# Rows of x stored tile by tile from SyncE's queue, and a group's gates by themselves

## The chip, the cores and the metric

The kernel runs on one core of a Trainium2 chip. The metric is the device time of one execution in microseconds (us). The engines of the core are TensorE (PE in the rows; its weight loads are PEld), VectorE (DVE), ScalarE (ACT), GpSimd (POOL) and SyncE (SP), which does nothing but issue transfers. Transfers (DMA) run on 16 DMA engines. SyncE's transfers form one hardware queue (q1 on the page), GpSimd's another one, made by software (q0).

## What is computed

Three layers in fp32, one after the other. Chunked attention (chunks of 64 tokens) gives the rows `x`, 4608 tokens of 512 numbers. A mixture of 8 experts takes one expert for each token that is not skipped and adds the expert's result, scaled with the gate. A last layer takes the maximum of three products and multiplies it with `w_out`.

```python
x = attn_out.transpose(0, 2, 1, 3).reshape(B * S, H * D)
e_idx = np.argmax(xc @ w_gate, axis=1)          # only where x @ w_skip > 0
gate_w = softmax(xc @ w_gate)[arange, e_idx]
y[mask] = gate_w[mask, None] * (np.maximum(xc[mask] @ w1[e], 0) @ w2[e])
out[do_compute] = xc + y
h = np.maximum(np.maximum(x @ w1, x @ w2), x @ w3)
return h @ w_out
```

## The kernel before

The first stage (up to about 165 us) is a loop over 36 tiles of 128 tokens, `for t in range(NT)`, in which the steps of several tiles overlap: round t loads q, k and v ahead, copies q and k into the order that TensorE wants (`pair_big`, on GpSimd), transposes them, makes the scores of tile t, transposes the exponentials of tile t-1, and multiplies those of tile t-2 with v. `scaled(t - 2)` then divides by the sums: on VectorE it writes the 128 rows of x of this tile (L361) into a buffer `xg` that holds the four tiles of a group, 128 x 4 x 520 numbers. The first tile of a group also has GpSimd clear the last seven columns of that buffer (L357). There are nine groups, and two such buffers: group 2 takes the buffer of group 0, group 3 that of group 1, and so on. `x_transpose(t - 2)` turns the rows for the routing (L374), and `logits` follows a round later.

When the four tiles of a group have their logits, `route(g)` and, a round later, `gates(g)` choose the experts; L432 writes the gate of each token into column 512 of the group's buffer. `store_x(g)` then writes the whole group, rows and gates, to `x_dram` with one transfer of GpSimd's (L546). In the rounds after that the slots of the group's tokens are sent with indirect transfers (`send_id`, L524), nine rounds after the tile. The ids so collected are read back by `load_ids` (L540) on SyncE: `ids_0` (the first columns of expert 0, wanted for the first gathers), the rest in `ids_sb`, and `ids_2` near the end. With these ids the second stage gathers rows of `x_dram` for each expert (L555); the first three tiles for expert 0 are gathered while the first stage still ends.

TensorE, VectorE, ScalarE and GpSimd run in the order in which the code is written (`manual_schedule`). SyncE's order is not written out: the scheduler places each transfer where its own model of time expects it to be ready. Each of SyncE's transfers uses one of eight completion semaphores in turn (DMAHW0 to DMAHW7 in the rows below), those of GpSimd DMASW0 to DMASW7.

A load of v of round t goes into one of eight buffers `v_all`, six rounds before it is used; loads of q and k go as far ahead.

Of the kernel before, what the change touches and what calls it, by code (L numbers as in the profile page):

```python
# [19 lines left out]
P = 128  # L20
B, H, S, D = 8, 8, 576, 64
N = B * S
DM = H * D
# [6 lines left out]
NT = N // P  # L30
# [10 lines left out]
def kernel(  # L41
# [15 lines left out]
    nc = tc.nc  # L57
# [5 lines left out]
    x_dram = dram.tile([N + 1, XW], F32, name="x_dram")  # L63
# [23 lines left out]
    def ps_sm(name):  # L87
        return ps("sm", name)
# [27 lines left out]
    def expert_src(e, i):  # L116
        if i < 4:
            return w1[e, i * P:(i + 1) * P, :], f"e{e}_{i}", (1, F1)
        r = (i - 4) * 2 * P
        return w2[e, r:r + 2 * P, :].rearrange("(a p) d -> p a d", p=P), f"e{e}_{i}", (2, DM)  # L120
# [67 lines left out]
    def pieces(t, end):  # L188
        got, t0 = [], t
        while t < end:  # L190
            b, s = divmod(t, WHOLE) if t < P * FULL else divmod(t - P * FULL, TAIL)
            n = min(end - t, (WHOLE if t < P * FULL else TAIL) - s)
            got.append((t - t0, b, s if t < P * FULL else s + WHOLE, n))
            t += n
        return got
# [54 lines left out]
    def load_v(t):  # L250
        for off, b, s, n in pieces(t * P, (t + 1) * P):
            link["load"] = nc.sync.dma_start(
                v_all[t % NV][off:off + n, :, :D], v[b, :, s:s + n, :].rearrange("h k d -> k h d"))
# [96 lines left out]
    def scaled(t):  # L350
        xp = units[t // 2]["xp", t % 2]
        g, j = PLACE[t]
        if j == 0:
            parts = [bpool.tile([P, GT, XW], F32, tag="xg", name=f"xg{g}")]
            groups[g] = parts, apool.tile([P, GT, E + 1], F32, tag="lg", name=f"lg{g}")
            for part in parts:
                nc.gpsimd.memset(part[:, :, DM + 1:], 0.0)  # L357
        sm = apool.tile([P, 2, 4], F32, tag="sm", name=f"sm{t}", bufs=3)
        nc.vector.tensor_scalar_add(sm, xp[:, :, :, D], 1e-9)
        nc.vector.reciprocal(sm, sm)  # L360
        nc.vector.tensor_tensor(  # L361
            rows_of(t)[:, :DM].rearrange("p (h r d) -> p r h d", h=4, r=2), xp[:, :, :, :D],
            sm.unsqueeze(3).to_broadcast([P, 2, 4, D]), op=ALU.mult)

    def rows_of(t):
        g, j = PLACE[t]
        part, i = divmod(j, groups[g][0][0].shape[1])
        return groups[g][0][part][:, i, :]
# [12 lines left out]
    def logits(t):  # L381
        g, j = PLACE[t]
        lp = ps_sm(f"lp{t}")[:, :R]
        for c in range(KC):
            link["logits", t] = nc.tensor.matmul(lp, xt[t][:, c, :], wcat[:, c, :], start=c == 0, stop=c == KC - 1)
        units["lp", t] = lp

    def logits_out(t):
        g, j = PLACE[t]
        nc.scalar.copy(groups[g][1][:, j, :], units["lp", t])  # L390
# [29 lines left out]
    def gates(g):  # L420
        parts, nt = groups[g][0], SIZES[g]
        T = slice(0, nt)
        ex, m8, comp = routing[g]
        oh, eo = picks[g]
        sm = apool.tile([P, GT], F32, tag="rsm", name=f"rsm_{g}", bufs=1)
        nc.vector.reduce_sum(sm[:, T], ex[:, T], axis=AX)
        nc.vector.tensor_scalar(eo[:, T], m8[:, T], float(-COLS), float(E * COLS + P * SLOTS), op0=ALU.mult, op1=ALU.add)
        nc.vector.tensor_scalar_add(sm[:, T], sm[:, T], 1e-9)
        nc.vector.scalar_tensor_tensor(eo[:, T], comp[:, T], float(-P * SLOTS), eo[:, T], op0=ALU.mult, op1=ALU.add)
        for i, part in enumerate(parts):  # L430
            n = part.shape[1]
            nc.vector.reciprocal(part[:, :, DM], sm[:, i * n:i * n + n])  # L432
        store_x(g)
        before, after = run[g % 2], run[(g + 1) % 2]
        got = apool.tile([P, E], F32, tag="rgot", name=f"rgot_{g}", bufs=1)
        nc.vector.reduce_sum(got, oh[:, T].rearrange("p t e -> p e t"), axis=AX)
        nc.vector.tensor_tensor(after, before, got, op=ALU.add)
# [101 lines left out]
    def load_ids(dst, which, cols, eng=nc.sync):  # L539
        follow(eng.dma_start(dst, ids_rows[which][:, cols]), sent[which], "slots are written in any order")  # L540

    def store_x(g):
        r = START[g] * P
        for part in groups[g][0]:
            n = part.shape[1] * P
            nc.gpsimd.dma_start(x_dram[r:r + n, :].rearrange("(t p) c -> p t c", p=P), part)  # L546
            r += n

    def apart(ins, own, other):
# [203 lines left out]
    def last_of(t):  # L753
        return PLACE[t][0] if 0 <= t < NT and PLACE[t][1] == GT - 1 else None

    def weights_ahead(t):
        for i, at, *_ in ROUND:
            if at == t:
                src, name, shape = expert_src(0, i)
                with tc.issue_after(link["load"].ins):  # L760
                    if i in STAGED:
                        a = shape[0]
                        nc.sync.dma_start(raws_0[i].rearrange("p (a b) -> p a b", a=a) if a > 1 else raws_0[i], src)
                    else:
                        raws_0[i] = load_raw(src, name, shape)
# [15 lines left out]
    for t in range(NT):  # L781
        u, s = divmod(t, 2)
        ranked = last_of(t - 5)
        if ranked is not None:
            rank_out(ranked)
        if t - LAG in late:
            send_id(t - LAG)
        if t == 0:
            load_qk(5)
        if s == 0 and u + 6 < SLOW + 2 * len(BIG):  # L790
            load_qk(u + 6)
        units.setdefault(u, {})
        if t >= 1 and t - 1 not in vm:
            cross(t - 1)
        if t == NT - 2:
            cross(NT - 2)
            cross(NT - 1)
        for group in PAIR.get(t, ()):
            (pair_big if len(group) > 2 else pair_heads)(*group[:2])
        if t == 8:  # L800
            nc.gpsimd.tensor_copy(tok_f, tok_i)
            nc.gpsimd.tensor_scalar_add(tok_f, tok_f, float(-N))
            nc.gpsimd.iota(col_i, pattern=[[1, P]], base=0, channel_multiplier=0)
            nc.gpsimd.tensor_copy(col_f, col_i)
        if t >= 2:
            values(t - 2)
            scaled(t - 2)
            if t - 2 + NV < NT:
                load_v(t - 2 + NV)
        weights_ahead(t)  # L810
        if t in (33, 34):
            with tc.issue_after(link["load"].ins):
                raws_1[EARLY[t - 33]] = load_raw(*expert_src(1, EARLY[t - 33]))
        scores(t)
        shift(t)
        if t >= 1:
            exp_transpose(t - 1)
        for group in TURN.get(t, ()):
            (turn_big if len(group) > 2 else qk_transpose)(*group[:2], "q")
        if t >= 1:  # L820
            cross_up(t - 1)
        if t >= 3:
            logits(t - 3)
            logits_out(t - 3)
        for group in TURN.get(t, ()):
            (turn_big if len(group) > 2 else qk_transpose)(*group[:2], "k")
        exponentials(t)
        g = last_of(t - 3)
        if g is not None:
            route(g)  # L830
        if t >= 2:
            x_transpose(t - 2)
            x_out(t - 2)
        g = last_of(t - 4)
        if g is not None:
            gates(g)
            rank_of(g)
        g = ranked
        if g is not None:
            if g == 2:  # L840
                count_first()
            place(g)
            if g == FIRST:
                late = range(START[g + 1], NT)
                fill_first(run[(g + 1) % 2][:, 0:1])
                xgs[0] = [four_kb([P, XW], F32, f"xg_0_{j}") for j in range(2)]
                rows = START[g + 1] * P
                fetch = t + 6
        if fetch is not None and t - fetch in (-4, -3):
            for i in range(2):  # L850
                send_id(START[FIRST] + 2 * (t - fetch + 4) + i)
            if t == fetch - 3:
                load_ids(ids_0, 0, slice(0, 3))
        rounded(t)
        rests(t)
        if t == fetch:
            at = cpool.tile([P, 2], I32, name="at")
            nc.vector.tensor_single_scalar(at, ids_0[:, :2], rows - 1, op=ALU.min)
            for j in range(2):
                gather(xgs[0][j], at[:, j:j + 1], rows)  # L860
# [5 lines left out]
        send_id(t)  # L866
    values(NT - 2)
    scaled(NT - 2)
    logits(NT - 3)
    logits_out(NT - 3)  # L870
    exp_transpose(NT - 1)
# [7 lines left out]
    load_ids(ids_sb, 0, slice(0, SLOTS))  # L879
    values(NT - 1)  # L880
    scaled(NT - 1)
    logits(NT - 2)
    logits_out(NT - 2)
    rounded(36)
# [450 lines left out]
    for b, (r0, n) in enumerate(BLOCKS):  # L1335
# [31 lines left out]
        for half in range(2):  # L1367
            for i in range(n // P):
# [11 lines left out]
                r = r0 + half * n + i * P  # L1380
# [34 lines left out]
```

## Time and profile before

| | us |
|---|---|
| median of 3 runs | 1050.54 (1046.76 to 1053.8) |
| the profiled execution | 1043.47 |
| its span, first to last instruction | 1041.8 |
| TensorE busy | 999.0 (96%) |
| VectorE busy | 575.4 (55%) |
| ScalarE busy | 420.2 (40%) |
| GpSimd busy | 315.6 (30%) |

Busy times are those of one profiled execution; its own time stands in the second row, beside the median of the runs that were timed. In a row of a timeline the first number is the start of the instruction in us from the span's start, the second its duration. The clock of TensorE is given as a share of full speed, 2.4 GHz; 0.50 is 1.2 GHz. The share of DMA is the mean busy share of the 16 engines, and can be over 1 where packets of two queues overlap.

### The profile page before, as it was taken

The page shows a single profiled execution, that of the slowest core. Times are in us where ns is not written, and L with a number is a line of the kernel's source. Part 1 is how long each engine was busy: PE and PEld are TensorE (multiplying, and loading weights), DVE is VectorE, ACT ScalarE, POOL GpSimd, SP SyncE. Part 2 cuts the span into 40 slices and gives each one's busy share as a digit, 9 for nine tenths or more (in the row PEclk, how much of TensorE's full clock was granted, in tenths as well). Part 3 has the DMA queues.
Part 4 walks back from the last instruction along what each step waited for, and adds up shares of the span by engine and source line. Part 5 has one row for each costly group of instructions (what it writes and reads, how often), then busy time and mean ns, then how long its engine had stood idle before and what let it go on. Part 6 is the DMA issues. An engine that isn't in the chain of part 4 may idle for free.

```text
span 1041.8 us, 19679 instructions
## 1 busy us (share of the span) xinstructions
PE 999.0 (96%) x7569; PEld 855.2 (82%) x7569; DVE 575.4 (55%) x1100; ACT 420.2 (40%) x762; POOL 315.6 (30%) x359
## 2 busy tenths in 40 slices
PE   8998999998989999899999999999999999999996
PEld 7988988888777888787878887788888888878995
DVE  4676888688273795655898524343344424434241
ACT  5876874455251554424443422223222322223230
POOL 3665867512120343105321502213012311103010
PEclk9998999999999999999999999999999999999999
DMA  9999973877281795659995446645566356674771
GB/s 235 295 307 293 238 237 111 260 248 272 87 284 62 250 329 200 234 188 349 339 319 169 149 142 185 192 132 172 162 193 190 103 168 200 185 222 156 224 232 40
DMA packets 198258, 217.44 MB, mean 209 GB/s; under 512 B 47195, under 2 KB 162027, under 8 KB 198144
## 3 DMA queue, kind: packets, MB, share of 16 engines
q1 hardware_dynamic: 185328, 176.27, 55.7%
q0 software_dynamic: 10224, 31.40, 8.7%
q10 hardware_dynamic: 2592, 8.26, 2.1%
q8 instruction: 70, 1.15, 0.5%
q14 instruction: 44, 0.36, 0.1%
HBM read 175.30 MB, written 41.98 MB: 209 GB/s over the span
## 4 chain that ended last, share of the span: by engine, by line
PE 51%; DMA 3%; DVE 2%; issue 0%; ACT 0%; SPq 0%; DVEq 0%; ACTq 0%
PE f_a L663 6%; PE f_a L665 6%; PE f_a L664 6%; PE o L663 5%; PE o L665 5%; PE o L664 5%; PE f_d L663 3%; PE f_d L665 3%; PE f_d L664 3%; DMA ws<-m_sums 2%; PE f_b L663 2%; PE f_b L665 2%; PE f_b L664 2%; PE trf L1124 1%; DMA x<-x_dram 1%; PE h L663 0%
## 5 line engine op out<-in xcount | busy, mean ns | idle before, releaser
L94 POOL TENSOR_TENSOR fh<-best,fh 128x512 fp32r<-128x512 f32 (+1 forms) x60 | 75.2, 1260 | 358.1 <-ACT fh L93 271.1
L663 PE MATMUL f_a<-x_t,ws 128*128 128x512 f32 (+1 forms) x270 | 100.3, 372 | 0.8 <-DVE best L1298 0.8
L665 PE MATMUL f_a<-x_t,ws 128*128 128x512 f32 (+1 forms) x270 | 99.6, 369 | 0.0
L664 PE MATMUL f_a<-x_t,ws 128*128 128x512 f32 (+1 forms) x270 | 99.5, 369 | 0.0
L664 PE MATMUL o<-wlo_m,fh 128*128 128x512 f32 x216 | 84.6, 392 | 0.0
L663 PE MATMUL o<-whi_m,fh 128*128 128x512 f32 x216 | 84.5, 392 | 0.0
L665 PE MATMUL o<-whi_m,fh 128*128 128x512 f32 x216 | 83.4, 393 | 0.0
L943 POOL DMA_INDIRECT x_dram<-xg,ids_sb x20 | 30.0, 1501 | 172.5 <-DVE xg L941 81.0
L93 ACT CAST whi_e<-raw_e 128x1024 fp32r<-128x1024 f32 x56 | 58.2, 1051 | 58.8 <-DMA raw_e<-in_moe_w_dram 39.0
L663 PE MATMUL h<-xhi,whi_e 128*128 128x256 f32 x256 | 73.5, 287 | 7.9 <-PEq L1240 2.8
L94 DVE TENSOR_TENSOR wlo_e<-raw_e,whi_e 128x1024 fp32r<-128x1024 f32 x56 | 68.0, 1222 | 20.6 <-ACT whi_e L93 20.2
L663 PE MATMUL y<-whi_e,hhi 128*128 128x512 f32 x184 | 74.0, 403 | 0.9 <-ACT hhi L1012 0.9
L93 ACT CAST fh<-best 128x512 fp32r<-128x512 f32 (+1 forms) x60 | 34.5, 579 | 95.0 <-DVE best L1300 58.3
L664 PE MATMUL h<-xlo,whi_e 128*128 128x256 f32 x256 | 72.5, 283 | 0.2 <-issue 0.2
L665 PE MATMUL y<-whi_e,hlo 128*128 128x512 f32 x184 | 72.5, 397 | 0.2
L665 PE MATMUL h<-xhi,wlo_e 128*128 128x256 f32 x256 | 72.5, 283 | 0.0
L664 PE MATMUL y<-wlo_e,hhi 128*128 128x512 f32 x184 | 72.2, 393 | 0.0
L1130 POOL TENSOR_TENSOR x_t<-t,x_t 128x512 fp32r<-128x512 f32 (+1 forms) x40 | 46.1, 1182 | 50.9 <-ACT x_t L1129 50.9
L1303 ACT COPY p<-f_a 128x512 f32<-128x512 f32 (+1 forms) x45 | 24.3, 543 | 87.0 <-PE f_a L665 86.8
L663 PEld LDWEIGHTS f_a<-x_t,ws 128*128 128x128 f32 x270 | 51.0, 189 | 9.9 <-DVE best L1298 1.6
L665 PEld LDWEIGHTS f_a<-x_t,ws 128*128 128x128 f32 x270 | 50.9, 189 | 8.6
L663 PEld LDWEIGHTS h<-xhi,whi_e 128*128 128x128 f32 x256 | 49.2, 192 | 10.7 <-issue 9.3
(242 smaller groups left out, 2604.8 us busy)
## 6 DMA issues: line engine op xcount, KB each, us to landing
ws<-m_sums SPq DMA_DIRECT2D x135, 512.0 KB
raw_e<-in_moe_w_dram SPq DMA_DIRECT2D x64, 512.0 KB
ws<-m_sums SPq DMA_DIRECT2D x45, 256.0 KB
x_dram<-xg POOLq DMA_DIRECT2D x9, 1040.0 KB, 6.5
x<-x_dram SPq DMA_DIRECT2D x36, 256.0 KB
v_all<-in_v_dram SPq DMA_DIRECT2D x32, 256.0 KB
out_dram<-os SPq DMA_DIRECT2D x32, 256.0 KB
m_sums<-n_raw ACTq DMA_DIRECT2D x18, 448.0 KB
```

The costliest lines, as they stand in the source:

```text
L93: nc.scalar.copy(hi, src),
L94: eng.tensor_tensor(lo, src, hi.bitcast(F32), op=ALU.subtract),
L663: nc.tensor.matmul(acc, ahi, bhi, start=first, stop=False, skip_group_check=onto)
L664: nc.tensor.matmul(acc, ahi, blo, start=False, stop=False, skip_group_check=onto)
L665: return nc.tensor.matmul(acc, alo, bhi, start=False, stop=last, skip_group_check=onto)
L943: ins = nc.gpsimd.indirect_dma_start(out=x_dram[:, :], out_offset=bass.IndirectOffsetOnAxis(ap=ids, axis=0), in_=xg, in_offset=None, bound ...
L1124: nc.tensor.transpose(tr[:, i * P:(i + 1) * P], row[:, c * P:(c + 1) * P], ident)
L1130: eng.tensor_tensor(lo, src, hi.bitcast(F32), op=ALU.subtract)
L1303: nc.scalar.copy(p1, acc_a)
```

## The change

`store_x(g)`, one transfer of 1040 KB for each group on GpSimd, is gone. In its place `store_tile(t)` writes the 512 columns of x of one tile (256 KB), on SyncE, and is called behind `scaled` of this tile, 36 times. `store_gates(g)` writes the last eight columns (the gate and the seven cleared ones) of a group's 512 rows, 16 KB in pieces of 32 bytes, on SyncE, at the place where `store_x` was called.

```diff
--- before.py
+++ after.py
@@ -430,7 +430,7 @@
         for i, part in enumerate(parts):
             n = part.shape[1]
             nc.vector.reciprocal(part[:, :, DM], sm[:, i * n:i * n + n])
-        store_x(g)
+        store_gates(g)
         before, after = run[g % 2], run[(g + 1) % 2]
         got = apool.tile([P, E], F32, tag="rgot", name=f"rgot_{g}", bufs=1)
         nc.vector.reduce_sum(got, oh[:, T].rearrange("p t e -> p e t"), axis=AX)
@@ -539,11 +539,15 @@
     def load_ids(dst, which, cols, eng=nc.sync):
         follow(eng.dma_start(dst, ids_rows[which][:, cols]), sent[which], "slots are written in any order")
 
-    def store_x(g):
+    def store_tile(t):
+        nc.sync.dma_start(x_dram[t * P:t * P + P, :DM], rows_of(t)[:, :DM])
+
+    def store_gates(g):
         r = START[g] * P
         for part in groups[g][0]:
             n = part.shape[1] * P
-            nc.gpsimd.dma_start(x_dram[r:r + n, :].rearrange("(t p) c -> p t c", p=P), part)
+            nc.sync.dma_start(
+                x_dram[r:r + n, DM:].rearrange("(t p) c -> p t c", p=P), part[:, :, DM:])
             r += n
 
     def apart(ins, own, other):
@@ -807,6 +811,7 @@
             scaled(t - 2)
             if t - 2 + NV < NT:
                 load_v(t - 2 + NV)
+            store_tile(t - 2)
         weights_ahead(t)
         if t in (33, 34):
             with tc.issue_after(link["load"].ins):
@@ -866,6 +871,7 @@
         send_id(t)
     values(NT - 2)
     scaled(NT - 2)
+    store_tile(NT - 2)
     logits(NT - 3)
     logits_out(NT - 3)
     exp_transpose(NT - 1)
@@ -879,6 +885,7 @@
     load_ids(ids_sb, 0, slice(0, SLOTS))
     values(NT - 1)
     scaled(NT - 1)
+    store_tile(NT - 1)
     logits(NT - 2)
     logits_out(NT - 2)
     rounded(36)
```

The scheduler places the new transfers in SyncE's line. These are SyncE's rows in the first stage, around the load of `v_all5` for tile 13, before (xg0 is the buffer of group 0, xg1 that of group 1):

```order
L252 DMA v_all4_138<-in_v_dram 128x8x64
L222 DMA qt10_927<-in_q_dram 128x4x256
L222 DMA kt10_928<-in_k_dram 128x4x256
L252 DMA v_all5_139<-in_v_dram 128x8x64
L222 DMA qt11_1121<-in_q_dram 128x4x256
L222 DMA kt11_1122<-in_k_dram 128x4x256
L252 DMA v_all6_140<-in_v_dram 128x8x64
L252 DMA v_all7_141<-in_v_dram 128x8x64
```

The same place after the change:

```order
L252 DMA v_all4_138<-in_v_dram 128x8x64
L543 DMA x_dram_66<-xg1_738 128x512
L222 DMA qt10_933<-in_q_dram 128x4x256
L222 DMA kt10_934<-in_k_dram 128x4x256
L252 DMA v_all5_139<-in_v_dram 128x8x64
L543 DMA x_dram_66<-xg1_738 128x512
L549 DMA x_dram_66<-xg0_374 128x4x8
L222 DMA qt11_1129<-in_q_dram 128x4x256
L222 DMA kt11_1130<-in_k_dram 128x4x256
L252 DMA v_all6_140<-in_v_dram 128x8x64
L543 DMA x_dram_66<-xg1_738 128x512
L252 DMA v_all7_141<-in_v_dram 128x8x64
```

Stores of tiles of group 0 (128x512, from xg0) and of group 1 (from xg1) now stand between the loads, and the gates of group 0 (L549, 128x4x8) stand two places behind the load of `v_all5`.

On VectorE the order stays. What changes is what tile 8, the first of group 2, waits for. Before (the names in brackets are semaphores):

```order
L359 TENSOR_SCALAR sm8_1151<-xp8_1131 128x8 [waits PE_49]
L360 RECIPROCAL sm8_1151<-sm8_1151 128x8 [waits DVE_49]
L361 TENSOR_TENSOR xg2_1148<-xp8_1131,sm8_1151 128x2x4x64 [waits DMASW5_49,DVE_49,Pool_49]
L313 TENSOR_REDUCE mx10_1173<-sc10_1156 128x8 [waits PE_49]
L315 TENSOR_TENSOR ex10_1175<-sc10_1156,mx10_1173 128x2x4x64 [waits DVE_49,Activation_49]
```

After:

```order
L359 TENSOR_SCALAR sm8_1159<-xp8_1139 128x8 [waits PE_49]
L360 RECIPROCAL sm8_1159<-sm8_1159 128x8 [waits DVE_49]
L361 TENSOR_TENSOR xg2_1156<-xp8_1139,sm8_1159 128x2x4x64 [waits DMAHW4_49,DMAHW3_49,DMAHW5_49,DMAHW1_49,DMAHW7_49,DVE_49,Pool_49]
L313 TENSOR_REDUCE mx10_1182<-sc10_1165 128x8 [waits PE_49]
L315 TENSOR_TENSOR ex10_1184<-sc10_1165,mx10_1182 128x2x4x64 [waits DVE_49,Activation_49]
```

L361 waited for one transfer of GpSimd's and now waits for five of SyncE's, the four stores of tiles of group 0 and its gates. The maxima of round 10 (L313) stand behind it, as before.

The last place is SyncE's line at the end of the first stage. Before:

```order
L100 DMA raw_e1_1_3557<-in_moe_w1_dram 128x1024
L540 DMA ids_0_121<-ids_dram0_67 128x3
L540 DMA ids_sb_118<-ids_dram0_67 128x288
L540 DMA ids_2_120<-ids_dram1_68 128x1
L616 DMA n_raw0_4513<-in_moe2_w1_dram 128x2x512
```

After:

```order
L100 DMA raw_e1_1_3590<-in_moe_w1_dram 128x1024
L540 DMA ids_0_121<-ids_dram0_67 128x3
L540 DMA ids_sb_118<-ids_dram0_67 128x288
L543 DMA x_dram_66<-xg7_3209 128x512 x2
L549 DMA x_dram_66<-xg6_2800 128x4x8
L543 DMA x_dram_66<-xg7_3209 128x512 x2
L543 DMA x_dram_66<-xg8_3582 128x512 x2
L549 DMA x_dram_66<-xg7_3209 128x4x8
L543 DMA x_dram_66<-xg8_3582 128x512
L540 DMA ids_2_120<-ids_dram1_68 128x1
L543 DMA x_dram_66<-xg8_3582 128x512
L549 DMA x_dram_66<-xg8_3582 128x4x8
```

The stores of tiles 28 to 34 (from xg7 and xg8) and the gates of groups 6 and 7 now stand behind the loads of `ids_0` and `ids_sb`, and the store of tile 35 and the gates of group 8 behind that of `ids_2`.

## Rows read from the trace of the kernel before

**Rows 1.** The page: span, and busy time of the engines.

```profile
span 1041.8 us, 19679 instructions
PE 999.0 (96%) x7569; PEld 855.2 (82%) x7569; DVE 575.4 (55%) x1100; ACT 420.2 (40%) x762; POOL 315.6 (30%) x359
```

**Rows 2.** Stretches: length, busy time (instructions) of each engine, clock, DMA.

```profile
core 0: us, PE busy (x) PEld busy (x) DVE busy (x) ACT busy (x) POOL busy (x), PEclk, DMA share, GB/s
...
40.00:64.00 24.00, 22.71 (x490) 21.50 (x489) 17.54 (x58) 18.09 (x41) 14.68 (x28) 1.00 1.04 296
...
92.00:99.00 7.00, 7.00 (x92) 6.55 (x90) 4.55 (x15) 3.58 (x9) 1.41 (x3) 0.51 1.02 247
```

**Rows 3.** Timeline of SyncE: start, duration of the issue, line, transfer.

```profile
27.76 2.50 SPq L222 DMA_DIRECT2D qt<-in_q_dram  x1
30.36 1.28 SPq L222 DMA_DIRECT2D kt<-in_k_dram  x1
...
57.56 1.06 SPq L252 DMA_DIRECT2D v_all<-in_v_dram  x1
...
72.26 1.64 SPq L100 DMA_DIRECT2D raw_e<-in_moe_w_dram  x1
...
89.84 1.57 SPq L100 DMA_DIRECT2D raw_e<-in_moe_w_dram  x1
...
156.09 0.34 SPq L540 DMA_DIRECT2D ids<-ids_dram  x1
...
175.27 0.32 SPq L540 DMA_DIRECT2D ids<-ids_dram  x1
```

**Rows 4.** Timeline of GpSimd; in brackets its idle time before, and what ended it.

```profile
34.79 0.61 POOL L233 COPY qr<-qt 128x512 f32<-128x512 f32 x1 [2.00 <-DMA qt<-in_q_dram]
36.89 0.61 POOL L233 COPY kr<-kt 128x512 f32<-128x512 f32 x1 [1.49 <-DMA kt<-in_k_dram]
...
44.70 0.78 POOL L546 DMA_DIRECT2D x_dram<-xg  x1
...
55.13 0.12 POOL L357 MEMSET xg<- 128x28 f32 x1 [0.26 <-DMA x_dram<-xg]
...
148.83 0.81 POOL L546 DMA_DIRECT2D x_dram<-xg  x1 [4.77 <-DVE run L437]
...
184.34 1.06 POOL L555 DMA_INDIRECT xg<-x_dram,ids  x1 [0.30 <-issue]
```

**Rows 5.** Timeline of VectorE, L361 of tiles 8, 12, 16 and 32.

```profile
55.20 0.69 DVE L361 TENSOR_TENSOR xg<-xp,sm 128x512 f32<-128x512 f32 x1 [0.54 <-DMA x_dram<-xg]
...
70.78 0.69 DVE L361 TENSOR_TENSOR xg<-xp,sm 128x512 f32<-128x512 f32 x1 [0.18 <-DMA x_dram<-xg]
...
88.48 0.69 DVE L361 TENSOR_TENSOR xg<-xp,sm 128x512 f32<-128x512 f32 x1
...
158.20 0.69 DVE L361 TENSOR_TENSOR xg<-xp,sm 128x512 f32<-128x512 f32 x1
```

**Rows 6.** Timeline of TensorE: tile 8 turned, and two idle times.

```profile
56.82 0.60 PE L374 MATMUL trx<-ident,xg 128*128 128x128 f32 x4
...
71.40 0.57 PE L306 MATMUL sc<-kT,qT 64*64 64x64 f32 x22 [1.26 <-issue]
...
90.88 0.21 PE L306 MATMUL sc<-kT,qT 64*64 64x64 f32 x1 [2.50 <-issue]
```

**Rows 7.** Waits of GpSimd to 150, TensorE to 156 us: total, times, longest.

```profile
POOL x_dram L546 <- DVE run L437: 20.1, 6, 4.8
...
PE sc L306 <- issue: 6.0, 4, 2.5
```

**Rows 8.** Instructions on x_dram: the stores, duration min/median/max, and the landing.

```profile
L546 POOL DMA_DIRECT2D x_dram<-xg x9: 778/802/821, 44.7 to 177.0; - x9
...
DMA to landing us min/median/max: 3.0/6.5/8.2
```

## The prediction

> **What bounds the kernel now.** I read the page first: the span is 1041.8 us and TensorE is busy in 999.0 of it [rows 1], so the kernel ends when TensorE's work ends, and the change can cost or bring only what it adds to or takes from TensorE's idle time. The change touches the first stage alone (attention and routing, up to about 185 us). There, the table of stretches says that the 16 DMA engines are full: from 40 to 64 us their share is 1.04 at 296 GB/s [rows 2]. The list of waits says who was late: GpSimd waited 20.1 us before its stores of x, always for `run` of L437, the end of the gates [rows 7], but that cost nothing, since none of TensorE's groups in that list waits for GpSimd: TensorE's idle time from 26 to 156 us stands in three groups there, all ended by nothing that the profile shows ("issue"), the largest 6.0 us in 4 places before the scores [rows 7]. The two largest are 1.26 us at 71.4 and 2.50 us at 90.9 [rows 6]; after the second the clock is at 0.51 from 92 to 99 [rows 2], which costs 7.0 x (1 - 0.51) = 3.4 us more. Last, the timelines of SyncE, GpSimd and VectorE give the times of the single steps [rows 3 to 5].
>
> The place to look at is the buffer of a group. `xg` has two buffers, so group 2 takes that of group 0, and neither its first scaled tile (L361, tile 8) nor its memset (L357) can start before the stores of group 0 have landed. Before, this is just met: GpSimd's store is issued at 44.70, and the memset at 55.13 and L361 at 55.20 come after a wait of 0.26 and 0.54 us for its landing [rows 4, 5]. For group 3 the wait is 0.18 us, at 70.78, for group 4 there is none [rows 5].
>
> **What the change removes.** Nine stores on GpSimd, 0.80 us each, 7.2 us together [rows 8], and the 20.1 us of waiting ahead of them. GpSimd's next work (slots' stores, copies of q, k and v) comes that much earlier, but nobody waited for it: 0. At the seam to the experts the same holds: the gather of the third tile starts at 184.34 right behind GpSimd's last send, with 0.30 us of idle time that ends by itself [rows 4], so an earlier store moves nothing. I put 0; the bound above is what GpSimd's rows before it hold, 0.80 us.
>
> **What it adds and moves.** 36 stores of 256 KB and 9 of 16 KB in SyncE's line, which is in order. The store of tile t waits for L361 of tile t only, the gates' for L432. The rows of the order show that the gates of group 0 now stand two places behind the load of `v_all5`, though what they hold is ready three of the loop's rounds before it is needed. And that load is issued only at 57.56 [rows 3], 2.4 us after the moment when group 2 needs the buffer. So SyncE's line runs behind the loop here, and GpSimd's own queue did not. This is the step on which the forecast rests:
> Issue: 57.56 + 1.06 for the load's own issue [rows 3] + about 0.4 for the store of tile 5 (the short issues are 0.32 to 0.34 [rows 3]) = 59.0. The line also carries more ahead of it: six tile stores, 6 x 0.262 = 1.57 MB, where the GpSimd store had moved 1.06 MB through the same engines; 0.51 MB more at 296 GB/s [rows 2] is 1.7 us. Bounds 59.0 (if two queues at once had cost the engines as much) and 60.7; I take 60.0.
> Landing: of SyncE's loads two show it, since GpSimd waited for them: issued at 27.76 and 30.36, used at 34.79 and 36.89 [rows 3, 4], so 7.0 and 6.5 us for half a megabyte, of which its own bytes are 0.52 / 296 = 1.8 us. Small gates behind a full line: 4.7 to 5.2. The gates are 512 pieces of 32 bytes, which no row before shows; the nearest is a load of v in 1024 pieces, whose issue took 1.06 us [rows 3], so half of that, 0.5 us, is in the bounds that follow. Below stands the shortest landing of any transfer of x_dram, 3.0 us [rows 8], above 7.0. I take 4.5.
> So group 0's gates land at 64.5 (62.0 to 67.7), and L361 of tile 8 starts there and not at 55.20: 9.3 us late (6.8 to 12.5).
>
> The Trainium skill's page "DMA: Bandwidth & Descriptors", section "Queues, rings and completion order", says that an engine takes one queue's descriptors in ring order and goes round robin between queues. By that rule the store in GpSimd's own queue passed the loads, and the gates in SyncE's cannot; the rows agree. The same page ("Anatomy of one DMA") prices a transfer at 2.0 us plus its bytes at 436 GB/s; by it the gates would land at 62.0 and the wait be 6.8 us, and the sum 6.5. The 6.5 and 7.0 us of the rows are longer, and they decide.
>
> What hangs on L361: VectorE works in order, so the maxima and differences of round 10 stand behind it; TensorE transposes tile 8 at 56.82, 0.9 us after L361 ends at 55.89 [rows 5, 6], and the next exponentials' transposes come behind that. Neither has more than that 0.9 us to give, and the DVE, ACT and PE steps of the next round start from L361 too. All 9.3 us are TensorE's.
>
> The clock: a gap of 2.50 us was followed by half the clock, 3.4 us [rows 2, 6]. One of 7 to 9 us can do the same; bounds 0 and 3.4, I take 2.6. Against it, the gaps of 1.26 and 2.50 us and the 3.4 us of half clock (7.2 in all) stand in the profile of before; after the stop SyncE's line is some 9 us nearer to the loop, so they may go. They end by no engine's work, and the engines stay as full as at 40 to 64 us, so I credit a little under half, 3.4; bounds 0 and 7.2.
>
> Later groups: the gates of group 1 stand behind the load issued at 72.26 [rows 3] and the store of tile 9: 72.26 + 1.64 + 0.4 + about 1 (the shift chosen above) + 4.5 = 79.8, needed at 70.78 + 9.3 = 80.1 [rows 5]. Those of group 2 stand behind 89.84 [rows 3]: 89.84 + 1.57 + 0.4 + 1 + 4.5 = 97.3, needed at 88.48 + 9.3 = 97.8. Both are met by the first stop, barely: 0.5 for the two together (0 to 3).
>
> Near the end, the stores of tiles 28 to 31 and the gates of group 6 stand behind the load of `ids_0`, issued at 156.09 [rows 3]. It waits for slots whose sends stood behind the megabyte store at 148.83 [rows 4]. Without this store they leave some 5 us earlier, so the gates land before L361 of tile 32 at 158.20 [rows 5]. If not, 156.09 + 0.8 + 3.0 = 159.9, 1.7 us late. I put 0. The store of tile 35 and the last gates stand behind `ids_2`, issued at 175.27 [rows 3]: 175.27 + 0.8 + 7.0 = 183.1 at the latest landing, before the gather at 184.34.
>
> **Sum**: 9.3 + 2.6 - 3.4 + 0.5 = +9.0 us. The profiled execution took 1043.47 us (the span and 1.7 us around it), so it would take 1052.5. It is 7.1 us under the median of the runs, 1050.54; on that the forecast is 1059.5. A measurement of this kernel tells about 1% (10.5 us) from no change, so this is just inside.
>
> **Rivals.** (1) The stop recurs. If tile stores cost the engines more than loads of the same size, the line falls further behind at groups 3 and 4. A store that takes 1.5 us in place of 0.9 adds 0.6 x 4 = 2.4 us a group, and with the first wait at its upper bound this is 12.5 + 2.4 + 2.4 + 2.6 - 3.4 = +16.5: 1067. For it: both later groups are met by under 1 us. Against: from group 2 on the loop is 9 us later, and so is every need.
> (2) The stop comes but is paid back: 6.8 + 0 - 7.2 = about 0, 1050. It needs TensorE's gaps to hang on how far SyncE's line is behind; nothing in the rows says so.
> (3) Faster. Without the megabyte bursts of GpSimd's queue the loads flow better, the gates land by 55.2, and the gaps of 71.4 and 90.9 go with their half clock: -7.2, 1043; with the other two places of the 6.0 us, -9.4. The point that decides is the landing of group 0's gates: 57.56 + 3.0 is over 55.2 already, so SyncE's line must be at least 5 us further at this place than it was, with more bytes in it. The same page of the Trainium skill ("Issuing engine by pattern") gives plain stores to SyncE as generally faster; no row here shows it for a line that is full.
> (4) No change at all, since the loop needs the buffer later than I read: excluded by the 0.54 us wait at 55.20.
>
> **How the numbers follow.** Forecast (one stop, +4 to +13): 0.68. Rival 1: 0.12. Rival 2: 0.12. Rival 3: 0.08. The range goes from rival 2 (1050) to rival 1 (1067). Over 1061.0 lie rival 1 and two fifths of the forecast: 0.40. Under 1040.0 lies most of rival 3: 0.06. The rest is 0.54.
>
> **What will show it.** VectorE's L361 of tile 8 and the memset ahead of it should end a wait of 7 to 12 us for a transfer of x_dram at 62 to 68 us, TensorE's largest gap in the first stage should be there, with half the clock behind it, and groups 3 to 8 should wait under 2 us each. The gather of the third tile should start 7 to 12 us after 184.34, and no wait of TensorE's should be new at the seam. The forecast is wrong if L361 of tile 8 starts before 60 us, if a later group's wait is longer than group 2's, or if SyncE is no longer behind the loop at `v_all5`.

## The result and the profile after

The changed kernel takes 1051.05 us (median of 22 runs), the kernel before 1046.1 us in the runs beside it (median of 22). The ratio of the two is 1.0077, 95% interval [1.0058, 1.0096]: of 1046.1 us that is 8.1 us (6.1 to 10.0). The plain difference of the two medians, 4.95 us, lies under that interval, so 5 to 8 us is taken for the cost below, and up to 10 can't be excluded. It is under the 1% that, by the prediction, a measurement tells from no change; over 22 runs of each kernel the interval excludes 1 all the same. The forecast was 1059.5, which is +9.0 us on the 1050.54 known then: of its 8.45 us too much, 4.4 are the change of the median before, and the rest is a sum that was some 1 to 4 us too high; against the interval alone, +9.0 is not off.

The profiled execution after took 1049.09 us, 5.6 more than that of before. The page after: span, busy times, and the two large queues (packets, MB, share of 16 engines).

```profile
span 1047.3 us, 19780 instructions
PE 999.4 (95%) x7569; PEld 856.0 (82%) x7569; DVE 573.9 (55%) x1100; ACT 419.8 (40%) x762; POOL 309.7 (30%) x350
...
q1 hardware_dynamic: 195264, 185.86, 57.7%
q0 software_dynamic: 7776, 21.81, 6.4%
```

TensorE's busy time is nearly the same, 999.4 us for 999.0 [rows 1], and the span is 5.5 us longer: by this page 5.1 of it is idle time. Work at the half clock counts as busy, for as long as it then takes, so the page doesn't show what the clock cost. SyncE's queue (q1) now carries the rows of x too. GpSimd's busy time fell by 5.9 us, which gained nothing.

The timeline of SyncE after (start, duration of the issue, line, transfer): the load of `v_all5`, the store of tile 5, the gates of group 0, then the gates of groups 1 and 2, and the load of `ids_0`.

```profile
56.25 1.03 SPq L252 DMA_DIRECT2D v_all<-in_v_dram  x1
57.37 1.46 SPq L543 DMA_DIRECT2D x_dram<-xg  x1
58.91 0.39 SPq L549 DMA_DIRECT2D x_dram<-xg  x1
...
73.03 0.38 SPq L549 DMA_DIRECT2D x_dram<-xg  x1
...
89.85 0.38 SPq L549 DMA_DIRECT2D x_dram<-xg  x1
...
153.71 0.34 SPq L540 DMA_DIRECT2D ids<-ids_dram  x1
```

Before, GpSimd had sent the rows and gates of group 0 at 44.70 [rows 4]. Now the gates of this group leave at 58.91, behind the load of `v_all5`, as the order had shown. GpSimd's timeline after: the last copy ahead of the memset, the memset of group 2's buffer, and the gather of the third tile.

```profile
53.03 0.61 POOL L233 COPY kr<-qkt 128x512 f32<-128x512 f32 x1
63.83 0.12 POOL L357 MEMSET xg<- 128x28 f32 x1 [10.18 <-DMA x_dram<-xg]
...
187.77 1.04 POOL L559 DMA_INDIRECT xg<-x_dram,ids  x1 [0.30 <-DVE hlo L706]
```

The memset ends a wait of 10.18 us for a transfer of `x_dram`, where before it had waited 0.26 us [rows 4]. So the gates landed at about 63.8, 4.9 us after their issue. VectorE's timeline after, L361 of tiles 8, 12, 16, 20, 32 and 35:

```profile
64.05 0.69 DVE L361 TENSOR_TENSOR xg<-xp,sm 128x512 f32<-128x512 f32 x1 [9.65 <-DMA qt<-in_q_dram]
...
82.78 0.69 DVE L361 TENSOR_TENSOR xg<-xp,sm 128x512 f32<-128x512 f32 x1
...
98.42 0.69 DVE L361 TENSOR_TENSOR xg<-xp,sm 128x512 f32<-128x512 f32 x1
...
114.47 0.69 DVE L361 TENSOR_TENSOR xg<-xp,sm 128x512 f32<-128x512 f32 x1 [0.23 <-DMA v_all<-in_v_dram]
...
161.70 0.69 DVE L361 TENSOR_TENSOR xg<-xp,sm 128x512 f32<-128x512 f32 x1
...
174.77 0.69 DVE L361 TENSOR_TENSOR xg<-xp,sm 128x512 f32<-128x512 f32 x1
```

The name in the first row's brackets is a load of q. SyncE's transfers share eight semaphores, and of several that an instruction waits for the view names one; that a store of group 0 ended the wait is read from GpSimd's memset, which needs the same buffer and came free 0.22 us earlier, and that this store was the gates is shown by the first two experiments. Against [rows 5], tile 8 is 8.85 us late, tile 12 12.0 late, tile 16 9.9, and tile 32 3.5. Tiles 20 and 35 are not in [rows 5]; the same line in VectorE's timeline before:

```profile
110.00 0.69 DVE L361 TENSOR_TENSOR xg<-xp,sm 128x512 f32<-128x512 f32 x1
...
169.97 0.69 DVE L361 TENSOR_TENSOR xg<-xp,sm 128x512 f32<-128x512 f32 x1
```

So tile 20 is 4.5 and tile 35 4.8 us late: the stop cost 8.85 us at once, the lateness grew to 12.0 over the next four tiles, and more than half was back by tile 20. Two views of TensorE after say why. Its timeline, the first work behind the stop, and its waits from 26 to 156 us (total, times, longest):

```profile
64.89 1.08 PE L374 MATMUL trx<-ident,xg 128*128 128x128 f32 x4 [8.17 <-DVE xg L361]
...
PE trx L374 <- DVE xg L361: 8.2, 1, 8.2
PE sc L306 <- issue: 1.0, 1, 1.0
```

and three stretches (length, busy time and instructions of PE, PEld, DVE, ACT and POOL, clock, DMA share, GB/s):

```profile
60.75:74.40 13.65, 9.51 (x141) 9.00 (x145) 6.93 (x24) 4.71 (x10) 5.25 (x9) 0.50 1.08 303
74.40:100.00 25.60, 25.60 (x584) 24.31 (x577) 19.85 (x61) 20.65 (x46) 15.45 (x27) 1.00 1.04 304
100.00:114.00 14.00, 13.98 (x337) 13.02 (x340) 11.71 (x38) 11.38 (x27) 10.27 (x15) 1.00 0.76 222
```

The new wait of 8.2 us is the only one worth the name. The clock was at 1.2 GHz from the middle of the stop to 74.4 us, and the 9.51 us of work done in that time would have taken about half as long at 2.4 GHz (four transposes of L374 take 1.08 us here and 0.60 at full clock [rows 6]): 4.8 us lost, an estimate. Against that, the 6.0 us of idle time "issue" before the scores [rows 7] became 1.0, and the half clock of 92 to 99 us [rows 2], worth 3.4, is not there. The account of the two profiles is 8.2 + 4.8 - 5.0 - 3.4 = +4.6 us, which is what tile 20 shows (4.5). One of the four idle places of before lies ahead of the stop, in TensorE's timeline before:

```profile
40.77 0.56 PE L306 MATMUL sc<-kT,qT 64*64 64x64 f32 x19 [1.14 <-issue]
```

This 1.1 us can't be the stop's doing; after the change TensorE has 1.0 us of such idle time before the transposes of q at 46.7 in its place. With that the sum is +5.6, so the account holds to about 1 us. Behind the stop 3.8 us of idle time and the 3.4 of the clock went, 7.2 together.

### The profile page after: what moved, and what is told of

It is laid out like the page before. It is cut to its first block, busy times and chain, and to the rows that moved or that the text cites. A ratio compares the mean times of both kernels' runs of the same rounds, so it can differ in the third digit from the quotient of the medians.

```text
span 1047.3 us, 19780 instructions
## 1 busy us (share of the span) xinstructions
PE 999.4 (95%) x7569; PEld 856.0 (82%) x7569; DVE 573.9 (55%) x1100; ACT 419.8 (40%) x762; POOL 309.7 (30%) x350
## 4 chain that ended last, share of the span: by engine, by line
PE 48%; DMA 5%; DVE 3%; issue 1%; ACT 1%; POOL 0%; SPq 0%; DVEq 0%; ACTq 0%; POOLq 0%
PE f_a L667 6%; PE f_a L669 6%; PE f_a L668 6%; PE o L667 5%; PE o L669 5%; PE o L668 5%; DMA ws<-m_sums 3%; PE f_d L667 3%; PE f_d L669 3%; PE f_d L668 3%; PE trf L1131 1%; PE f_b L667 1%; PE f_b L668 1%; PE f_b L669 1%; DMA x<-x_dram 1%
```

## The experiments

**Theory A**: SyncE's line is behind the loop where the gates of groups 0 and 1 stand, these hold a group's buffer of a megabyte until they have landed, and the loop stops, once, at the first such place. **Rival B**: what costs is the load on SyncE's line, 45 more transfers, 36 of them of 256 KB. **Rival C**: it is a matter of the start alone, the first group, and the rest of the change costs nothing or brings something. **Rival D**: the split into small stores costs, on whichever queue. Each kernel below is timed against the kernel before on the same chip; the first four share one median of it, 1050.68 us, the last two another, 1042.23.

**1. Gates in a small tile of their own.** All 45 stores stay on SyncE; only the buffer that the gates hold is another one, so that `xg` comes free when its last tile has been stored.

```diff
-            for part in parts:
-                nc.gpsimd.memset(part[:, :, DM + 1:], 0.0)
+            own_gates[g] = apool.tile([P, GT, XW - DM], F32, tag="gates", name=f"gates{g}", bufs=3)
+            nc.gpsimd.memset(own_gates[g][:, :, 1:], 0.0)
...
-            nc.vector.reciprocal(part[:, :, DM], sm[:, i * n:i * n + n])
+            nc.vector.reciprocal(own_gates[g][:, :, 0], sm[:, i * n:i * n + n])
...
-                x_dram[r:r + n, DM:].rearrange("(t p) c -> p t c", p=P), part[:, :, DM:])
+                x_dram[r:r + n, DM:].rearrange("(t p) c -> p t c", p=P), own_gates[g])
```

> All stores of the change stay on SyncE. Only the gates (and the seven cleared columns) of a group get a small tile of their own, three buffers of 128x4x8, so that the buffer of x no longer waits for the gates' store. Theory A (group 2 waits for group 0's gates, which stand in SyncE's late line): L361 of tile 8 starts at 55 to 56 us as in the kernel before, since only the four tile stores hold the buffer; no gap of TensorE over 1.5 us between 50 and 70; time within 0.3% of the kernel before. Rival B (the line itself costs: 45 more transfers and 512 small pieces a group delay the loads): the wait at L361 goes, but TensorE stops elsewhere in the first stage and the time stays 0.6 to 1.0% above before.

Measured: 1051.98 us beside 1050.68, ratio 1.0012 [0.9979, 1.0045]. VectorE's L361 of tiles 8 and 12, then the gates of group 0 in SyncE's timeline:

```profile
54.35 0.69 DVE L361 TENSOR_TENSOR xg<-xp,sm 128x512 f32<-128x512 f32 x1
...
72.01 0.69 DVE L361 TENSOR_TENSOR xg<-xp,sm 128x512 f32<-128x512 f32 x1
...
58.56 0.40 SPq L549 DMA_DIRECT2D x_dram<-gates  x1
```

The gates leave as late as with the change (58.56 for 58.91), but nothing waits for them, and the cost is gone within the interval, which ends under that of the change. TensorE's longest wait from 26 to 156 us is 1.4 us in this kernel, so it didn't stop elsewhere either. The same queue with the same transfers is therefore free, to within this interval, once its late gates hold no buffer of the loop; the four stores of tiles still hold the group's buffer here, and tile 8 doesn't wait for them: rival B falls.

**2. The gates on GpSimd's queue.** The tiles stay on SyncE.

```diff
-            nc.sync.dma_start(
+            nc.gpsimd.dma_start(
                 x_dram[r:r + n, DM:].rearrange("(t p) c -> p t c", p=P), part[:, :, DM:])
```

> The tile stores stay on SyncE as in the change; all gates' stores (16 KB a group) go to GpSimd's queue, where the whole store was before. Theory A: the gates are issued at 43 to 45 us and land in some 3 to 6 us, L361 of tile 8 starts at 55 to 56, and the time is within 0.3% of before. Rival B: 0.6 to 1.0% above before, since SyncE's line is nearly as long as in the change (36 of the 45 transfers).

Measured: 1047.9 us, ratio 0.9989 [0.9956, 1.0022]. GpSimd's timeline, the gates of group 0 and the memset of group 2:

```profile
46.06 0.78 POOL L549 DMA_DIRECT2D x_dram<-xg  x1
...
56.19 0.12 POOL L357 MEMSET xg<- 128x28 f32 x1
```

The buffer is the same as with the change, and so are the 36 stores of tiles on SyncE; only the nine small transfers go by the other queue, 12.9 us earlier for group 0. They left 1 us later than the 43 to 45 expected, and tile 8 came at 56.35, 0.35 late. Neither stop nor cost is left.

**3. Group 0 as before, groups 1 to 8 as in the change.**

```diff
     def store_tile(t):
-        nc.sync.dma_start(x_dram[t * P:t * P + P, :DM], rows_of(t)[:, :DM])
+        g = PLACE[t][0]
+        if not (g == 0):
+            nc.sync.dma_start(x_dram[t * P:t * P + P, :DM], rows_of(t)[:, :DM])
...
+            if g == 0:
+                nc.gpsimd.dma_start(x_dram[r:r + n, :].rearrange("(t p) c -> p t c", p=P), part)
+            else:
```

> Group 0 is stored as before (one transfer on GpSimd), groups 1 to 8 as in the change. Theory A, since SyncE's line stays some 13 us late as long as nothing stops the loop: L361 of tile 8 at 55 to 56, but the stop moves to group 3, which needs group 1's gates: they are issued at 72 to 75, land at 76 to 80, L361 of tile 12 starts there and not at 70.8, and the time is 0.4 to 0.9% above before. Rival C (only the crowded start at group 0 counts): L361 of tile 12 at 70 to 72, time within 0.3% of before.

Measured: 1054.41 us, ratio 1.0044 [1.0017, 1.0072]. VectorE's L361 of tiles 8 and 12, the gates of group 1 in SyncE's timeline, and the first of TensorE's waits from 26 to 156 us:

```profile
55.14 0.69 DVE L361 TENSOR_TENSOR xg<-xp,sm 128x512 f32<-128x512 f32 x1
...
80.93 0.69 DVE L361 TENSOR_TENSOR xg<-xp,sm 128x512 f32<-128x512 f32 x1 [8.34 <-POOL xg L357]
...
74.30 0.38 SPq L554 DMA_DIRECT2D x_dram<-xg  x1
...
PE trx L374 <- DVE xg L361: 6.9, 1, 6.9
```

With group 0 out of the way, the stop moves to tile 12, where group 3 wants the buffer of group 1. Its gates leave at 74.30, 3.5 us after the 70.78 at which tile 12 had started before [rows 5], and tile 12 starts 6.6 us after this issue. The view puts the wait of tile 12 down to GpSimd's memset, and that of the memset (8.43 us) to nothing that the profile shows; that the gates ended it is read from their place in the line and from the first experiment, where tile 12 starts at 72.01 behind the same stores of tiles. There is one stop again and no second one: no other wait of TensorE's up to 156 us is over 1 us. Rival C would have had no stop here, so it falls in this form: the first group is not special, it only comes first.

**4. Only group 0 as in the change, groups 1 to 8 as before** (the same edit with `g > 0` in place of `g == 0`).

> Only group 0 is stored as in the change (four tile stores and the gates on SyncE), groups 1 to 8 as before on GpSimd. Theory A: L361 of tile 8 starts at 61 to 65, the gap of TensorE before tile 8 is turned is 6 to 9 us, no later group waits over 1 us, and the time is 0.5 to 1.0% above before, as with the whole change. Rival B: the cost grows with the number of stores, so at most 0.2%.

Measured: 1058.92 us, ratio 1.0076 [1.004, 1.0111]. The gates of group 0 in SyncE's timeline, GpSimd's memset of group 2, the wait of TensorE, and two stretches (columns as above):

```profile
56.74 1.38 SPq L554 DMA_DIRECT2D x_dram<-xg  x1
...
62.29 0.12 POOL L357 MEMSET xg<- 128x28 f32 x1 [5.45 <-DMA x_dram<-xg]
...
PE trx L374 <- DVE xg L361: 4.2, 1, 4.2
...
40.00:65.00 25.00, 19.17 (x344) 17.66 (x347) 11.76 (x35) 13.38 (x29) 12.00 (x24) 0.86 1.09 301
65.00:75.00 10.00, 9.47 (x169) 8.89 (x161) 7.28 (x28) 6.01 (x15) 4.08 (x7) 0.83 1.15 313
```

One ninth of the change, four stores of tiles and one of gates, gives a cost that can't be told from that of the whole (1.0077). TensorE's wait is only half of the 8.2 us there, and under the 6 to 9 expected; the clock was lowered around it too, but what fills the other half is not settled by this profile. The half clock stands in it also from 99 to 106 and from 153.5 to 161 us, 3.4 us each, far behind the stop; no experiment shows whether the stop draws it there. Together with the third kernel this is the one stop of the theory: either group makes it, and with both it comes once.

**5. The whole group's store on SyncE, not split**, at the place of the gates.

```diff
     def store_tile(t):
-        nc.sync.dma_start(x_dram[t * P:t * P + P, :DM], rows_of(t)[:, :DM])
+        pass
...
-                x_dram[r:r + n, DM:].rearrange("(t p) c -> p t c", p=P), part[:, :, DM:])
+                x_dram[r:r + n, :].rearrange("(t p) c -> p t c", p=P), part)
```

> The rows aren't split: each group's whole store, rows and gates in one transfer of 1040 KB, goes to SyncE's queue where the change has the gates, and there are no stores of single tiles. In SyncE's line the store of group 0 stands right behind the load of v_all5. Theory A (what SyncE's line holds is late there, and with it the buffer of the group): the store is issued at 57 to 59 us and its megabyte lands 6.5 to 8.2 us later, so VectorE's L361 of tile 8 starts at 64 to 67 us (55.20 before, 64.05 with the change) behind a wait for x_dram, TensorE has a gap of 8 to 11 us there, tile 12 is 10 to 14 us late, and the ratio to before is 1.006 to 1.012. Rival D (the split into 36 stores of tiles and 9 of pieces of 32 bytes is what costs): L361 of tile 8 starts before 58 us and the ratio is 0.998 to 1.003.

Measured: 1053.56 us beside 1042.23, ratio 1.01 [1.0053, 1.0147]. The store of group 0 in SyncE's timeline, the memset and L361 of tile 8:

```profile
54.92 1.25 SPq L549 DMA_DIRECT2D x_dram<-xg  x1
...
62.98 0.12 POOL L357 MEMSET xg<- 128x28 f32 x1 [7.41 <-DMA x_dram<-xg]
...
63.05 0.69 DVE L361 TENSOR_TENSOR xg<-xp,sm 128x512 f32<-128x512 f32 x1 [8.11 <-DMA x_dram<-xg]
```

The store left 2 to 4 us earlier than expected, in a line without stores of tiles, and its megabyte took 8.1 us to land, at the upper end of the expected 6.5 to 8.2; tile 8 starts 1 us under the expected range and the cost lies inside it. TensorE's wait is 6.6 us in this profile, under the 8 to 11 expected. Without any split the stop is there: rival D falls.

**6. All 45 stores on GpSimd's queue.** Both calls of the change with `nc.gpsimd` in place of `nc.sync`.

> The split of the change, 36 stores of tiles and 9 of gates, all of them on GpSimd's queue instead of SyncE's. Theory A: the gates of group 0 are issued within 2 us of 44.70, when GpSimd issued the store before, so L361 of tile 8 starts at 55 to 57 us, that of tile 12 at 71 to 74, no TensorE gap is over 3 us in the first stage, and the ratio to before is 0.997 to 1.004. It may show waits of GpSimd's own, since 36 more issues of 0.8 us (29 us in all) stand between its copies of q and k; if these were late, gaps of TensorE's would be spread over the whole first stage. Rival D (the split costs, on whichever queue): the ratio is 1.006 or more, with a wait for x_dram at tile 8 or 12.

Measured: 1044.98 us beside 1042.23, ratio 1.0018 [0.9984, 1.0052]. The gates of group 0 in GpSimd's timeline, and L361 of tiles 8 and 12:

```profile
45.69 0.77 POOL L549 DMA_DIRECT2D x_dram<-xg  x1
...
54.73 0.69 DVE L361 TENSOR_TENSOR xg<-xp,sm 128x512 f32<-128x512 f32 x1
...
71.87 0.69 DVE L361 TENSOR_TENSOR xg<-xp,sm 128x512 f32<-128x512 f32 x1
```

The split costs nothing, to within the interval, on a queue that is not late. The 36 more issues were 0.56 us each and not 0.8, and GpSimd had the time. None of the six is faster than the kernel before by more than the interval.

**All eight profiles together.** L361 of tile 16, the first of group 4, in the six experiments in their order:

```profile
89.66 0.69 DVE L361 TENSOR_TENSOR xg<-xp,sm 128x512 f32<-128x512 f32 x1
...
89.30 0.69 DVE L361 TENSOR_TENSOR xg<-xp,sm 128x512 f32<-128x512 f32 x1
...
97.84 0.69 DVE L361 TENSOR_TENSOR xg<-xp,sm 128x512 f32<-128x512 f32 x1
...
97.96 0.69 DVE L361 TENSOR_TENSOR xg<-xp,sm 128x512 f32<-128x512 f32 x1
...
98.87 0.69 DVE L361 TENSOR_TENSOR xg<-xp,sm 128x512 f32<-128x512 f32 x1
...
89.12 0.69 DVE L361 TENSOR_TENSOR xg<-xp,sm 128x512 f32<-128x512 f32 x1
```

The four kernels without the stop are there at 88.48 [rows 5] to 89.66 and the four with it at 97.84 to 98.87, 9 us apart, whichever group made it. From there on the profiles differ in ways that are not explained here: tile 20 stands at 107.76 to 112.94 without it and at 114.47 to 119.77 with it, and tile 35 in experiments 1 and 2, which cost nothing, starts at 175.33 and 179.72 for 169.97 before. So one pair of profiles can't say to a few us what came back behind tile 16.

## Why the prediction was right

**The stop** was the step on which it rested, and it came as forecast: the gates' issue at 58.91 (60.0 taken, 59.0 to 60.7), landing 4.9 us later (4.5 taken), tile 8 at 64.05 (64.5 taken). The two misses cancelled in part, which is luck; TensorE felt 8.2 us of it, for the 9.3 taken. The issue was at the lower bound since the 0.51 MB more in SyncE's line had not made it later: the load of `v_all5` left at 56.25, 1.3 us earlier than before [rows 3]. That fits the reason given for the lower bound, that two queues at once had cost the engines as much, but no experiment was made on it. The store of tile 5 took 1.46 us to issue where 0.4 was taken, which gave most of this back. The rival price beside it, 2.0 us plus the bytes, of the Trainium skill's page "DMA: Bandwidth & Descriptors" ("Anatomy of one DMA"), which the page fits to GpSimd's path, would by that estimate have had the gates land at 61.0, 2.0 us behind their issue. The 4.9 us measured on SyncE's full line are more than twice as long, and the measurement decides. The 4.7 to 5.2 us worked out from the loads of q and k [rows 3, 4] were nearer.

**The half clock behind the stop** was undersized for this profile: 2.6 us (at most 3.4) taken from the one example of before, measured 4.8. It lasted 13.65 us and not 7.0, and began while TensorE was still idle. It varies: here are the stretches of half clock of experiments 3 and 5 (columns as above).

```profile
78.50:85.35 6.85, 3.58 (x71) 3.17 (x72) 4.11 (x13) 1.33 (x3) 3.64 (x6) 0.50 1.15 321
...
59.30:76.40 17.10, 12.51 (x173) 11.88 (x173) 9.87 (x32) 5.65 (x12) 5.28 (x9) 0.50 1.09 309
```

Half of the busy time is 1.8 and 6.3 us; in experiment 4 it is 2.6 (5.10 us of work from 61.60 to 68.45). **What went in exchange** was undersized too: 3.4 taken (at most 7.2), measured 7.2 behind the stop in this pair of profiles, the "issue" idle time and the half clock together, and 8.4 with the place at 40.8. But it can't all be put down to the stop. Experiment 6 has no stop, and the idle time that in the kernel before came ahead of the half clock of 92 to 99 us; yet its clock stays full, in TensorE's timeline and the stretch of 75 to 100 us:

```profile
91.51 0.21 PE L306 MATMUL sc<-kT,qT 64*64 64x64 f32 x1 [2.50 <-issue]
...
75.00:100.00 25.00, 21.40 (x518) 20.02 (x518) 17.03 (x62) 17.63 (x40) 17.60 (x30) 1.00 1.06 308
```

So the 3.4 us of before can be missing without a stop, and a gap of 2.50 us is not always followed by half the clock, as the term of 2.6 had taken from one example. The argument against the exchange, that the engines stay as full, holds as such (a DMA share of 1.04 from 74 to 100 us, as in [rows 2]) but did not decide. **The later groups** waited for nothing, 0 where 0.5 was taken: the gates of group 1 left at 73.03 and those of group 2 at 89.85, 9.8 and 8.6 us ahead of tiles 12 and 16. Their margin is larger than I worked out, as the loop was 12.0 and 9.9 us late by then and not 9.3, and as these gates left 2.3 and 3.0 us earlier than the 75.3 and 92.8 of my sums.

So the terms of the two profiles add up to +4.6 to +5.6, where tile 20 shows 4.5 and the spans 5.5, not to +9.0; the repeated runs say 5 to 8. That the sum came near is in part luck: the stop was 1 us smaller than taken, the clock behind it 2 larger, the exchange 4 to 5 larger and the later groups 0.5 smaller. Since 8.2 + 4.8 were lost in the profile, 5 to 8 us less than that were seen, an estimate from these rows that takes the profile's loss for all runs. That this part varies is seen in the other traces: TensorE's idle time "issue" before the scores, from 26 to 156 us, is 6.0, 6.2 and 5.9 us in the three kernels without the stop (experiments 1, 2 and 6), and with a stop 1.0 (the change), 4.3, 6.8 and 4.1 (experiments 3, 4 and 5). In one profile nearly all of it is gone, in the others a third or nothing. What makes this idle time come or go is open; no engine's work ends it, and no experiment here was made on it.

**At the end of the stage** no new wait came, as forecast: `ids_0` was loaded 2.4 us earlier than before in spite of the stop (153.71 for 156.09 [rows 3]), which fits the reason given, that GpSimd's megabyte store is gone from ahead of the sends. The clock is another matter: it was at 0.51 from 169.95 to 173.40 in this profile, where 3.34 us of work lost 1.6, and full there before; experiments 1, 2 and 6, without the stop, have such a stretch between 165 and 182 us too, so it needs no stop. The gather of the third tile came 3.4 us later than before, and not the 7 to 12 that I had named as a sign: that sign was set from the +9 of the sum, and in this profile more than half was back by then.

**The rivals.** That the stop recurs (1067) was excluded by the margins of groups 1 and 2; the third experiment shows that this is the shift of the first stop at work, since without it group 1's gates stop the loop. That it is paid back in full (+0) fails on the repeated runs, whose interval of the ratio excludes 1, but it was nearer than I gave it credit for: 7.2 of 13.0 us went behind the stop in the pair of profiles. The faster case fell at the point named for it: the gates left at 58.91, when tile 8 would have needed them landed by 55.2.

## What to carry to other kernels

When a store moves to another queue, ask what else stands in that queue ahead of it and when that is issued, and then which buffer the store holds: 16 KB of gates that left 14 us later than the old store held a megabyte's buffer and stopped TensorE for 8.2 us. The remedy is to part the two, by sending what holds the buffer through a queue that is not late, or by keeping the late part in a small tile of its own; both cost nothing here, to within 0.2% and 0.5%. The price of a stop is not its length: 8.2 us drew 4.8 us of slow clock with them in the profile, while the repeated runs cost 5 to 8, so that some of the 13 was made good elsewhere (why is open); and by shifting all later needs the stop kept the next late transfers from making a second one. One pair of profiles settles where a stop is and what it waits for, but not a sum of a few us: that takes repeated runs.

## What the runs showed of the hardware

Four things had not been expected. The half clock (1.2 GHz) began inside the stop, at 60.75, while TensorE was idle, before its next work at 64.89, and went on through 9.5 us of work behind it, until 74.40. A transfer of 16 KB in pieces of 32 bytes took 4.9 us to land behind SyncE's full line, and in experiment 5 one of 1040 KB 8.1 us: the smaller one saves 3.1 us for 1/65 of the bytes. The issue of these small pieces on SyncE took 0.39 us after the change, where the forecast had allowed for 0.5, but 1.38 in experiment 4. Stores of single tiles cost GpSimd 0.56 us each, under the 0.80 of the whole group's [rows 8]; that row's times stand in the sixth kernel's view of `x_dram`:

```profile
L543 POOL DMA_DIRECT2D x_dram<-xg x36: 540/564/641, 25.6 to 176.0; - x36
```
